# Attention with mirrored score blocks: another order of the key pairs in the middle chunks, later block writes, earlier v loads

## The chip, the cores and the metric

One core of a Trainium2 chip runs the whole program. The metric is the device time of one execution in microseconds; three runs of the kernel before are given, and one profiled execution with its trace. Engines are named as in the profile: PE (matmul), PEld (weight load), DVE (vector), ACT (scalar), POOL and SP (which here issues nearly all DMAs).

## The reference, cut to what matters

```python
# u, v: (8, 2496, 256); z: (8, 2496, 64)
scores = (1.0 / S) * np.matmul(z, z.transpose(0, 2, 1))
attn = np.maximum(scores, 0.0) ** 2
out = np.matmul(attn, v)
x = (u * out).reshape(B * S, D)
# then a mixture of 8 experts over the rows of x: argmax gate, at most 80 rows per expert,
# out[tok] = gate * (relu(x[tok] @ w1[e]) @ w2[e]), the other rows are zero
```

Per batch the matrix of scores is symmetric, since the same z stands on both sides.

## The kernel before

A batch has 2496 rows, padded to 20 tiles of 128 (NT). Queries are taken in 5 chunks of 4 tiles (512 columns, the last 448); keys in 10 pairs of two tiles (NP). A step is one (batch, chunk, pair), 400 in all, and the body of the loop over steps is the program order of PE, ACT, DVE and SP, written out by hand (`manual_schedule`), so each of these engines takes its work in the order in which the loop names it.

For a pair, `scores` (line 301) makes the two operands `ah` and `al` (the squared relu of the scores, rounded, and the rest), two steps ahead of their use (LOOK). There are three kinds of pair in chunk qc:

- *Mirrored*, keys of an earlier chunk j < qc: the block was made transposed when chunk j was the query. ACT casts it from the block `blk` that was read back (line 296), DVE subtracts (line 298, recorded at line 54). PE does nothing.
- *Diagonal*, keys of chunk qc: four score matmuls on PE (lines 312, 313), two relus and a square on ACT (316, 317), cast on DVE (107), subtract on DVE.
- *For later*, keys of a later chunk: the same, with the cast on ACT (line 105; on DVE for the entries of ON_V when b > 0), and `mirror` (line 252): DVE transposes both tiles into `x` (257, pool of NX = 4). After the fourth tile of a block SP writes `x` to DRAM as `y` (261).

The score tiles `s` in PSUM have three banks, two per pair; the operand `a` has two buffers, `ah` and `al` three.

`mirror_back` (265), once per step, reads blocks back with four DMAs each (278) into one of NA = 4 slots, in the order in which they will be used: two steps after their write was issued, at most AHEAD = 12 steps before `scores` uses them, and as soon as a slot is free.

`attend` (330) does a tile's matmuls into the chunk's two accumulators: per half three (343 to 345), for the last tile two (347, 348). A pair is 12 matmuls, the last pair 10.

Beside this each step has extra work at fixed positions r of the chunk: at r = 0 `chunk_x` for the chunk before (DVE, line 362), then ACT's first cast of it (`chunk_hi`, 373); r = 1 the rest on DVE (377) and the transposing store (SP, 412); r = 2 ACT's second cast (381); r = 3 the third part (385); r = 6 the logits (436, 444). The gate of a batch stands in the next batch's chunk 0 at r = 7 (463 to 478) and r = 8 (489 to 504), its counts in chunk 1 at r = 2 and 4 (513, 520). At r = 1 the next batch's z and the next `zd` are loaded (100, 120, 121), at r = 9 `prep_zc` (112). v of the next batch goes through two raw buffers: two loads in chunk 3 at r = 8, casts (146) in chunk 4 at r = 2, 4, 6, 8, 9, each followed by the load of a later group (132). In batch 0 the v groups are loaded and cast in chunk 0. In batch 7 the experts' first weights are loaded and split in chunks 2 to 4 (589, 599, 600).

Of the kernel before, what the change touches and what calls it, by code (L numbers as in the profile page):

```python
# [8 lines left out]
F32 = mybir.dt.float32  # L9
# [16 lines left out]
def attn_moe_kernel(ctx, tc, zT, uT, v, wg, w1, w2, out, seq, cap):  # L26
# [5 lines left out]
    nc = tc.nc  # L32
    V = nc.vector
    B, _, SP = zT.shape
# [3 lines left out]
    NT = SP // P  # L38
# [3 lines left out]
    QT = 4  # L42
    NQ = NT // QT
# [9 lines left out]
    def tt(o, a, b, op):  # L53
        V.tensor_tensor(out=o, in0=a, in1=b, op=op)  # L54
# [9 lines left out]
    dram = ctx.enter_context(tc.tile_pool(name="dram", bufs=1, space=DRAM))  # L64
# [3 lines left out]
    SQ = 32  # L68
# [58 lines left out]
    def load_v(b, g):  # L127
        last = g == NQ - 1
        nf = QT - 1 if last else QT
        raw = zpool.tile([P, QT, D], F32, tag="vraw", name=f"vraw_{b}_{g}")  # L130
        r0 = g * CH
        nc.sync.dma_start(out=raw[:, :nf],
                          in_=v[b, r0:r0 + nf * P, :].rearrange("(t p) d -> p t d", p=P))
        if last:

            r1 = r0 + nf * P
            for h in range(2):
                nc.sync.dma_start(out=raw[h * 64:(h + 1) * 64, nf], in_=v[b, r1:r1 + TAIL, :])
        return raw
# [93 lines left out]
    def zero_out(i, n):  # L233
# [3 lines left out]
                          in_=zero.rearrange("p (o d) -> p o d", o=1).broadcast_to([P, r1 - r0, D]))  # L237


    LOOK, AHEAD = 2, 12  # L240
    a_t = {}

# [1 line left out]

    half_t, y_t, blk, slot_of, free = {}, {}, {}, {}, list(range(NA))
    n32 = P // SQ
    now = [0]

    to_read = [(b, i, j, ((b * NQ + i) * NT + j * QT) // 2 - LOOK)
               for b in range(B) for i in range(NQ) for j in range(i)]  # L250

    def mirror(b, i, j, t, a):

        if t == 0:
            half_t[b, i, j] = sqpool.tile([P, n32, QT, QT, SQ], F32, tag="x", name=f"x_{b}_{i}_{j}")
        x = half_t[b, i, j]
        V.transpose(out=x[:, :, :, t].rearrange("p n k s -> p k n s"), in_=a)  # L257
        if t < QT - 1:
            return
        y = dram.tile([n32, SQ, n32, QT * QT * SQ], F32, tag="y", name=f"y_{b}_{i}_{j}", bufs=12)  # L260
        nc.sync.dma_start(out=y.rearrange("g p h f -> (g p) (h f)"),
                          in_=x.rearrange("p h k t s -> p (h k t s)"))
        y_t[b, i, j] = y, now[0]

    def mirror_back():

# [15 lines left out]
    def pair_tile(tag, b, qc, k, dt=F32R, bufs=3):  # L282
        return ew.tile([P, 2, CH], dt, tag=tag, name=f"{tag}_{b}_{qc}_{k}", bufs=bufs)
# [17 lines left out]
    def scores(b, qc, k):  # L301

        if k // QT < qc:
            return mirrored(b, qc, k)
        nq = min(CH, seq - qc * CH)
        zc, zd = zc_t[b, qc], zd_t[b, qc]
        a = pair_tile("a", b, qc, k, F32, 2)
        ss = []
        for h in range(2):
            zk = zc_t[b, k // QT][:, (k % QT + h) * P:(k % QT + h + 1) * P]  # L310
            s = ps_s.tile([P, CH], F32, tag="s", name=f"s_{b}_{qc}_{k + h}")
            nc.tensor.matmul(s[:, :nq], zk, zc[:, :nq], start=True, stop=False)  # L312
            nc.tensor.matmul(s[:, :nq], zk, zd[:, :nq], start=False, stop=True)  # L313
            ss.append(s)
        for h, s in enumerate(ss):
            nc.scalar.activation(out=a[:, h, :nq], in_=s[:, :nq], func=AF.Relu)  # L316
        nc.scalar.activation(out=a[:, :, :nq], in_=a[:, :, :nq], func=AF.Square)  # L317
        ah = pair_tile("ah", b, qc, k)
        on_v = k // QT == qc or (qc, k) in ON_V and b > 0
        cp(V if on_v else nc.scalar, ah[:, :, :nq], a[:, :, :nq])  # L320
        al = pair_tile("al", b, qc, k)
        tt(al[:, :, :nq], a[:, :, :nq], ah[:, :, :nq], ALU.subtract)
        if k // QT > qc:
            for h in range(2):
                mirror(b, k // QT, qc, k % QT + h, a[:, h])
        a_t[b, qc, k] = (ah, al)
# [2 lines left out]

    def attend(b, qc, k, cols=range(DC)):  # L330
        nq = min(CH, seq - qc * CH)
        if k == 0:
            acc_t[b, qc] = [ps_a.tile([P, CH], F32, tag="acc", name=f"acc_{b}_{qc}_{c}")
                            for c in range(DC)]
        acc = acc_t[b, qc]
        ah, al = (x[:, k % 2, :nq] for x in a_t[b, qc, k - k % 2])
        vt = v_t[b, k // QT]
        t = k % QT
        for c in cols:
            cs = slice(c * P, (c + 1) * P)  # L340
            o = acc[c][:, :nq]
            if k < NT - 1:
                nc.tensor.matmul(o, vt[:, t, 0, cs], ah, start=k == 0, stop=False)  # L343
                nc.tensor.matmul(o, vt[:, t, 1, cs], ah, start=False, stop=False)  # L344
                nc.tensor.matmul(o, vt[:, t, 0, cs], al, start=False, stop=False)  # L345
            else:
                nc.tensor.matmul(o, vt[:, t, 0, cs], ah, start=False, stop=False)
                nc.tensor.matmul(o, vt[:, t, 0, cs], al, start=False, stop=True)


    xt_t, xq_t, lg_t = {}, {}, {}
# [256 lines left out]
        ts(pre["half"], incl[:, :, NBLK - 3], -15.5, ALU.add)  # L608


    NP = NT // 2

    ON_V = {(0, 8), (0, 12), (0, 16)}

    early = [(e, w, part) for e in range(2) for w in (1, 2) for part in range(2)]
    qa, qb, qz = NQ - 3, NQ - 2, NQ - 1
# [4 lines left out]
    WARM = 4, 12  # L621
    steps = [(b, qc, r) for b in range(B) for qc in range(NQ) for r in range(NP)]
    ET = mybir.EngineType
    v_raw, z_raw, w_raw = {}, {}, {}
# [68 lines left out]
    with tc.manual_schedule(engines={ET.PE, ET.Activation, ET.DVE, ET.SP}):  # L693
        prep_zc(0, 0, raw0)
        prep_zd(0, 0, raw0)
        prep_zc(0, 1, raw12[:, 0])
        scores(0, 0, 0)
        prep_v(0, 0, vraw0, nc.scalar, V)
        scores(0, 0, 2)
        v_raw[0, 1] = vraw1  # L700
        z_raw.update({(0, 2): raw12[:, 1], (0, 3): raw34[:, 0], (0, 4): raw34[:, 1]})
        constants()
        prev = None
        for i, (b, qc, r) in enumerate(steps):
            last = b == B - 1 and qc == NQ - 1
            now[0] = i
            if r == 0 and prev:
                chunk_x(*prev)
            if (b, qc) == (0, 0) and r in (0, 2, 4):
                prep_zc(0, r // 2 + 2, z_raw.pop((0, r // 2 + 2)))  # L710
            if i + LOOK < len(steps):
                nb, nqc, nr = steps[i + LOOK]
                scores(nb, nqc, 2 * nr)
            if b == 0 and qc == 0:
                if r % 2 == 0 and r < 8:
                    g = r // 2 + 1
                    prep_v(0, g, v_raw.pop((0, g)), nc.scalar, V)
                    if g + 1 < NQ:
                        v_raw[0, g + 1] = load_v(0, g + 1)
                if r == 8:  # L720
                    constants_v()
            for k in (2 * r, 2 * r + 1):
                if not last or k < NT - 3:
                    attend(b, qc, k)
            if prev:
                finished(*prev, r)

            nb, nqc = (b, qc + 1) if qc + 1 < NQ else (b + 1, 0)
            if r == 2:
                prep_u(b, qc)  # L730
            if b + 1 < B:
                if r == 1:
                    z_raw[b + 1, qc] = load_z(b + 1, qc)
                if r == 9:
                    prep_zc(b + 1, qc, z_raw.pop((b + 1, qc)))
                if qc == NQ - 2 and r == 8:
                    for g in range(2):
                        v_raw[b + 1, g] = load_v(b + 1, g)
                if qc == NQ - 1:
                    g = (r - 1) // 2 if r < 9 else 4  # L740
                    if r in (2, 4, 6, 8, 9):
                        prep_v(b + 1, g, v_raw.pop((b + 1, g)), nc.scalar, V)
                        if g + 2 < NQ:
                            v_raw[b + 1, g + 2] = load_v(b + 1, g + 2)
            if nb < B and r == 1:
                prep_zd(nb, nqc)
            if r == 5:
                zero_out(b * NQ + qc, B * NQ)
            if b == B - 1 and qc >= NQ - 3:
                weights_ahead(qc, r)  # L750
            mirror_back()
            if r == NP - 1:
                prev = b, qc

        chunk_tiles(*prev)
        for kk, c in ((3, 0), (2, 0), (3, 1), (1, 0), (2, 1), (1, 1)):
            attend(*prev, NT - kk, [c])
            if kk == 1:
                chunk_x_last(*prev, c)
        chunk_store(*prev)  # L760
        chunk_logits_last(*prev)
        gate_top(b, NQ - 1, NQ)
        gate(b, NQ - 1, NQ)
        chunk_store2(*prev)
        kb = B * BPB
        count_last(kb - 2, kb)
        blocks(ps_m, "m", gp, oh, kb - 2, kb)
# [546 lines left out]
```

## Time and profile before

| | us |
|---|---|
| three runs, median (lowest to highest) | 1445.17 (1442.82 to 1446.08) |
| the profiled execution's own time | 1441.15 |
| its span on the core | 1439.4 |
| PE busy | 1385.3 (96%) |
| PEld busy | 1135.8 (79%) |
| DVE busy | 1074.9 (75%) |
| ACT busy | 983.1 (68%) |
| mean granted clock of PE | 0.991 |

Attention ends at about 1347 us; the rest is the experts. Busy times are unions of the instructions' recorded spans; ends of matmuls are modelled, so PE can be recorded as busy over short pauses, and pauses are better read from the starts. In the views by stretch, "us" is the length of the stretch, followed by busy time and number of instructions for PE, PEld, DVE, ACT and POOL, the granted clock as a share of full speed, and the busy share and rate of the DMA engines.

### The profile page before, as it was taken

Reading aid. Unit: us, or ns where it says so; the run is one execution under the profiler, and the core shown is the slowest. Engines: PE = TensorE matmul, PEld = TensorE weight load, DVE = VectorE, ACT = ScalarE, POOL = GpSimd, SP = SyncE. Lnnn points to the kernel's source line nnn. Section 1 sums busy time; section 2 is a strip of 40 time slices with the busy share of each in tenths; the row PEclk is TensorE's granted clock in tenths of the full one; section 3 lists DMA queues with packets and bytes.
Section 4 is the critical chain, followed back from the end, with each engine's and each line's share of the span. In section 5 each row is a group of like instructions: output and inputs, shape, how many; then the busy total and the mean of one; then the engine's idle time right before and its main releaser. Section 6 shows DMA issues by size and latency. Waiting matters only on the chain. (4 is left out here: it accounts for less than half of the span.)

```text
span 1439.4 us, 19509 instructions
## 1 busy us (share of the span) xinstructions
PE 1385.3 (96%) x7086; PEld 1135.8 (79%) x7086; DVE 1074.9 (75%) x1530; ACT 983.1 (68%) x1263; POOL 47.5 (3%) x48
## 2 busy tenths in 40 slices
PE   8999999999999999999999999999999999999687
PEld 6788877888788887888788877888878888887466
DVE  7766788667877688677877678767887678766784
ACT  8776677767776587756676577766776667766264
POOL 0000000000000000000000000000000000000075
PEclk9999999999999999999999999999999999999899
DMA  6799978996999959997899959999598979999944
GB/s 203 207 227 223 242 198 209 239 243 157 236 247 222 251 157 216 263 213 210 232 210 237 241 156 235 240 230 259 152 233 237 240 159 238 235 231 253 207 147 134
DMA packets 300103, 311.98 MB, mean 217 GB/s; under 512 B 136184, under 2 KB 228224, under 8 KB 289760
## 3 DMA queue, kind: packets, MB, share of 16 engines
q1 hardware_dynamic: 299040, 309.11, 86.3%
q0 software_dynamic: 960, 1.56, 0.4%
q8 instruction: 57, 0.93, 0.3%
q14 instruction: 46, 0.38, 0.1%
HBM read 153.48 MB, written 126.46 MB: 194 GB/s over the span
## 5 line engine op out<-in xcount | busy, mean ns | idle before, releaser
L345 PE MATMUL acc<-al,vt 128*128 128x512 f32 (+1 forms) x1520 | 587.5, 386 | 7.3 <-DVE al L54 7.1
L343 PE MATMUL acc<-ah,vt 128*128 128x512 f32 (+1 forms) x1520 | 586.9, 386 | 6.3 <-ACT ah L296 4.0
L344 PE MATMUL acc<-ah,vt 128*128 128x512 f32 (+1 forms) x1520 | 586.0, 386 | 1.2 <-DVE vt L146 1.2
L54 DVE TENSOR_TENSOR al<-a,ah 128x1024 fp32r<-128x1024 f32 (+1 forms) x240 | 291.2, 1213 | 143.8 <-ACT ah L105 134.2
L345 PEld LDWEIGHTS acc<-al,vt 128*128 128x128 f32 x1520 | 285.7, 188 | 66.8 <-DVE al L54 14.4
L343 PEld LDWEIGHTS acc<-ah,vt 128*128 128x128 f32 x1520 | 285.8, 188 | 63.5 <-ACT ah L296 7.4
L344 PEld LDWEIGHTS acc<-ah,vt 128*128 128x128 f32 x1520 | 285.9, 188 | 55.1 <-DVE vt L146 2.0
L316 ACT ACTIVATE a<-s 128x512 f32<-128x512 f32 (+1 forms) x480 | 257.6, 588 | 83.1 <-PE s L313 73.4
L296 ACT CAST ah<-blk 128x1024 fp32r<-128x1024 f32 x160 | 166.9, 1048 | 163.0 <-DMA blk<-y 81.7
L54 DVE TENSOR_TENSOR al<-blk,ah 128x1024 fp32r<-128x1024 f32 x160 | 193.0, 1214 | 93.0 <-ACT ah L296 90.5
L317 ACT ACTIVATE a<-a 128x1024 f32<-128x1024 f32 (+1 forms) x240 | 253.0, 1054 | 7.6
L257 DVE STREAM_TRANSPOSE x<-a 128x512 f32<-128x512 f32 x320 | 207.6, 686 | 0.0
L313 PE MATMUL s<-zd,zc 128*128 128x512 f32 (+1 forms) x480 | 186.9, 389 | 0.0
L105 ACT CAST ah<-a 128x1024 fp32r<-128x1024 f32 x139 | 146.0, 1050 | 4.4
L312 PE MATMUL s<-zc,zc 128*128 128x512 f32 x320 | 131.3, 410 | 3.5 <-ACT a L316 3.4
L107 DVE CAST ah<-a 128x1024 fp32r<-128x1024 f32 (+1 forms) x101 | 68.6, 679 | 46.6 <-ACT a L317 46.6
L313 PEld LDWEIGHTS s<-zd,zc 128*128 128x128 f32 x480 | 90.4, 188 | 15.4 <-issue 0.5
L373 ACT CAST xb<-xf 128x1024 bf16<-128x1024 f32 (+1 forms) x39 | 40.1, 1027 | 57.3 <-DVE xf L362 57.2
L312 PEld LDWEIGHTS s<-zc,zc 128*128 128x128 f32 x320 | 60.1, 188 | 21.8 <-ACT a L316 11.8
L312 PE MATMUL s<-zc 128*128 128x512 f32 (+1 forms) x160 | 63.8, 399 | 7.7 <-ACT a L316 7.6
L146 DVE TENSOR_TENSOR vt<-vraw,vt 128x1024 fp32r<-128x1024 f32 (+1 forms) x40 | 46.7, 1167 | 27.8 <-ACT vt L105 27.6
L105 ACT CAST vt<-vraw 128x1024 fp32r<-128x1024 f32 (+3 forms) x56 | 44.9, 828 | 30.9 <-DMA vraw<-v 30.9
(161 smaller groups left out, 843.3 us busy)
## 6 DMA issues: line engine op xcount, KB each, us to landing
y<-x SPq DMA_DIRECT2D x80, 1024.0 KB, 5.4
blk<-y SPq DMA_DIRECT2D x320, 256.0 KB, 8.3
out<-idle SPq DMA_DIRECT2D x40, 512.0 KB, 9.3
vraw<-v SPq DMA_DIRECT2D x32, 512.0 KB, 8.4
ut<-uT SPq DMA_DIRECT2D x32, 512.0 KB, 5.4
xs<-xq SPq DMA_DIRECT2D x32, 512.0 KB, 7.6
wraw<-w SPq DMA_DIRECT2D x28, 512.0 KB, 6.1
zd<-zc SPq DMA_DIRECT2D x78, 128.0 KB, 3.5
```

What stands on the lines that cost most here:

```text
L54: V.tensor_tensor(out=o, in0=a, in1=b, op=op)
L105: eng.copy(out=o, in_=i)
L107: eng.tensor_copy(out=o, in_=i)
L257: V.transpose(out=x[:, :, :, t].rearrange("p n k s -> p k n s"), in_=a)
L296: nc.scalar.copy(out=natural(ah), in_=src)
L312: nc.tensor.matmul(s[:, :nq], zk, zc[:, :nq], start=True, stop=False)
L313: nc.tensor.matmul(s[:, :nq], zk, zd[:, :nq], start=False, stop=True)
L316: nc.scalar.activation(out=a[:, h, :nq], in_=s[:, :nq], func=AF.Relu)
L317: nc.scalar.activation(out=a[:, :, :nq], in_=a[:, :, :nq], func=AF.Square)
L343: nc.tensor.matmul(o, vt[:, t, 0, cs], ah, start=k == 0, stop=False)
L344: nc.tensor.matmul(o, vt[:, t, 1, cs], ah, start=False, stop=False)
L345: nc.tensor.matmul(o, vt[:, t, 0, cs], al, start=False, stop=False)
```

## The change

Chunks 1 to 3 take their pairs in another order: those for later chunks, then the two diagonal ones, then the mirrored ones; chunks 0 and 4 keep theirs. `attend` starts and stops the accumulators at the first and last pair of that order, and `mirror_back`'s due times follow it. The write of a block is named by `mirror_out`, two steps after its last transpose, instead of in `mirror`. The first two v loads of the next batch move from chunk 3's r = 8 to r = 2 and r = 4. ON_V keeps one of three entries, so the casts of pairs 6 and 8 of chunk 0 go from DVE to ACT. Lines that only move are left out.

```diff
+    NP = NT // 2
+    pairs_of = [list(range(NP)) if qc in (0, NQ - 1) else
+                [*range(2 * qc + 2, NP), 2 * qc, 2 * qc + 1, *range(2 * qc)] for qc in range(NQ)]
...
-    now = [0]
-
-    to_read = [(b, i, j, ((b * NQ + i) * NT + j * QT) // 2 - LOOK)
+    now, to_write = [0], []
+
+    to_read = [(b, i, j, (b * NQ + i) * NP + pairs_of[i].index(2 * j) - LOOK)
                for b in range(B) for i in range(NQ) for j in range(i)]
...
-        y = dram.tile([n32, SQ, n32, QT * QT * SQ], F32, tag="y", name=f"y_{b}_{i}_{j}", bufs=12)
-        nc.sync.dma_start(out=y.rearrange("g p h f -> (g p) (h f)"),
-                          in_=x.rearrange("p h k t s -> p (h k t s)"))
-        y_t[b, i, j] = y, now[0]
+        to_write.append((now[0], b, i, j, x))
+
+    def mirror_out():
+
+        while to_write and to_write[0][0] + 2 <= now[0]:
+            _, b, i, j, x = to_write.pop(0)
+            y = dram.tile([n32, SQ, n32, QT * QT * SQ], F32, tag="y", name=f"y_{b}_{i}_{j}", bufs=12)
+            nc.sync.dma_start(out=y.rearrange("g p h f -> (g p) (h f)"),
+                              in_=x.rearrange("p h k t s -> p (h k t s)"))
+            y_t[b, i, j] = y, now[0]
...
-        if k == 0:
+        first, last = 2 * pairs_of[qc][0], 2 * pairs_of[qc][-1] + 1
+        if k == first:
...
-                nc.tensor.matmul(o, vt[:, t, 0, cs], ah, start=k == 0, stop=False)
+                nc.tensor.matmul(o, vt[:, t, 0, cs], ah, start=k == first, stop=False)
                 nc.tensor.matmul(o, vt[:, t, 1, cs], ah, start=False, stop=False)
-                nc.tensor.matmul(o, vt[:, t, 0, cs], al, start=False, stop=False)
+                nc.tensor.matmul(o, vt[:, t, 0, cs], al, start=False, stop=k == last)
...
-    ON_V = {(0, 8), (0, 12), (0, 16)}
+    ON_V = {(0, 8)}
...
-                scores(nb, nqc, 2 * nr)
+                scores(nb, nqc, 2 * pairs_of[nqc][nr])
...
-            for k in (2 * r, 2 * r + 1):
+            p = pairs_of[qc][r]
+            for k in (2 * p, 2 * p + 1):
...
-                if qc == NQ - 2 and r == 8:
-                    for g in range(2):
-                        v_raw[b + 1, g] = load_v(b + 1, g)
+                if qc == NQ - 2 and r in (2, 4):
+                    g = r // 2 - 1
+                    v_raw[b + 1, g] = load_v(b + 1, g)
...
             mirror_back()
+            mirror_out()
```

## Rows read from the trace of the kernel before

**Rows 1.** The page's busy time, share of the span and instructions of each engine.
```profile
PE 1385.3 (96%) x7086; PEld 1135.8 (79%) x7086; DVE 1074.9 (75%) x1530; ACT 983.1 (68%) x1263; POOL 47.5 (3%) x48
```

**Rows 2.** By stretch: chunk 2 of batch 0, chunk 3 of batch 1.
```profile
84.35:117.29 32.94, 32.94 (x168) 27.18 (x166) 23.01 (x29) 23.10 (x29) 0.00 (x0) 1.00 0.86 227
...
283.16:314.29 31.13, 31.13 (x160) 25.68 (x158) 20.45 (x25) 18.59 (x23) 0.00 (x0) 1.00 1.06 221
```

**Rows 3.** By stretch: 36 wide matmuls, then 60 narrow ones.
```profile
616.32:624.48 8.16, 8.16 (x37) 6.76 (x36) 5.83 (x8) 3.03 (x3) 0.00 (x0) 1.00 1.02 222
647.45:659.61 12.16, 12.16 (x62) 11.27 (x60) 10.23 (x12) 7.02 (x7) 0.00 (x0) 1.00 0.98 283
```

**Rows 4.** By stretch: chunk 4, chunks 0 and 1, batch 7's end.
```profile
sum 216.48, PE 207.60 PEld 183.96 DVE 154.94 ACT 141.16 POOL 0.00; mean PE 29.66 PEld 26.28 DVE 22.13 ACT 20.17 POOL 0.00
...
1177.69:1247.35 69.66, 69.64 (x351) 56.52 (x349) 59.53 (x94) 54.34 (x73) 0.00 (x0) 1.00 0.80 200
sum 497.81, PE 491.90 PEld 394.81 DVE 422.89 ACT 379.76 POOL 0.00; mean PE 70.27 PEld 56.40 DVE 60.41 ACT 54.25 POOL 0.00
...
1313.19:1347.00 33.81, 27.74 (x152) 22.66 (x150) 24.97 (x41) 18.30 (x23) 0.00 (x0) 1.00 0.97 238
```

**Rows 5.** Batch 0, order of time (start, us, engine, line); one stretch.
```profile
42.08 0.49 PE L343 MATMUL acc<-ah,vt 128*128 128x512 f32 x1 [2.27 <-ACT vt L105]
...
46.83 0.40 PE L344 MATMUL acc<-ah,vt 128*128 128x512 f32 x1
...
32.59 0.45 SPq L132 DMA_DIRECT2D vraw<-v  x1
...
43.20:46.60 3.40, 3.40 (x9) 2.67 (x10) 1.06 (x2) 3.34 (x4) 0.00 (x0) 0.53 1.09 287
```

**Rows 6.** Who waited for whom, whole span: us in total, times, longest.
```profile
SPq L261 <- DVE x L257: 324.1, 58, 16.4
...
ACT ah L296 <- DMA blk<-y: 81.7, 23, 5.7
```

**Rows 7.** Batch 5, chunk 4, order of time on SP and ACT.
```profile
994.71 0.41 SPq L132 DMA_DIRECT2D vraw<-v  x1
...
1002.14 1.04 ACT L105 CAST vt<-vraw 128x1024 fp32r<-128x1024 f32 x1 [4.98 <-DMA vraw<-v]
```

**Rows 8.** Batch 3, chunks 0 and 1, order of time on ACT.
```profile
544.17 0.34 ACT L467 ACTIVATE ex<-d 128x160 f32<-128x160 f32 x1 [3.07 <-DVE d L54]
...
554.13 1.05 ACT L373 CAST xb<-xf 128x1024 bf16<-128x1024 f32 x1 [3.57 <-DVE xf L362]
555.09 1.08 ACT L316 ACTIVATE a<-s 128x512 f32<-128x512 f32 x2
...
563.76 1.05 ACT L105 CAST ah<-a 128x1024 fp32r<-128x1024 f32 x1
...
566.92 1.05 ACT L105 CAST ah<-a 128x1024 fp32r<-128x1024 f32 x1
```

**Rows 9.** Batch 3, chunks 0 and 1, order of time on DVE.
```profile
541.14 1.23 DVE L54 TENSOR_TENSOR al<-a,ah 128x1024 fp32r<-128x1024 f32 x1 [0.36 <-ACT ah L105]
...
543.50 0.28 DVE L463 TENSOR_REDUCE mx<-lg 128x20 f32<-128x160 f32 x1
...
548.72 0.31 DVE L489 TENSOR_SCALAR_CACHE_REDUCE fw<-d 128x160 f32<-128x160 f32 x1
...
550.56 1.17 DVE L54 TENSOR_TENSOR al<-blk,ah 128x1024 fp32r<-128x1024 f32 x1
...
552.81 1.29 DVE L362 SCALAR_TENSOR_TENSOR xf<-acc,ut 128x512 f32<-128x512 f32 x2
...
570.67 2.02 DVE L54 TENSOR_TENSOR incl<-incl,tot 128x8 f32<-128x8 f32 x10
```

**Rows 10.** Batch 3, chunk 1, order of time on PE.
```profile
547.59 0.50 PE L343 MATMUL acc<-ah,vt 128*128 128x512 f32 x1 [0.69 <-ACT ah L296]
...
555.73 0.50 PE L312 MATMUL s<-zc,zc 128*128 128x512 f32 x1 [0.19 <-ACT a L316]
```

More of the change, by code (lines that the diff above doesn't have):

```diff
@@ L342, in attend @@
             if k < NT - 1:
-                nc.tensor.matmul(o, vt[:, t, 0, cs], ah, start=k == 0, stop=False)
+                nc.tensor.matmul(o, vt[:, t, 0, cs], ah, start=k == first, stop=False)
                 nc.tensor.matmul(o, vt[:, t, 1, cs], ah, start=False, stop=False)
-                nc.tensor.matmul(o, vt[:, t, 0, cs], al, start=False, stop=False)
+                nc.tensor.matmul(o, vt[:, t, 0, cs], al, start=False, stop=k == last)
             else:
                 nc.tensor.matmul(o, vt[:, t, 0, cs], ah, start=False, stop=False)
-                nc.tensor.matmul(o, vt[:, t, 0, cs], al, start=False, stop=True)
+                nc.tensor.matmul(o, vt[:, t, 0, cs], al, start=False, stop=k == last)
     xt_t, xq_t, lg_t = {}, {}, {}
@@ L608, in half @@
         ts(pre["half"], incl[:, :, NBLK - 3], -15.5, ALU.add)
-    NP = NT // 2
-    ON_V = {(0, 8), (0, 12), (0, 16)}
+    ON_V = {(0, 8)}
     early = [(e, w, part) for e in range(2) for w in (1, 2) for part in range(2)]
```

## The prediction

> **What bounds the kernel now.** I read the page's busy times first, then the busy time by stretch, then who waits for whom, then the order of time on each engine around the waits.
>
> PE is busy for 96% of the span [rows 1]. Whether it is the bound in a stage shows in the stretches: chunk 2 takes 32.94 us with 32.94 busy, chunk 3 takes 31.13 with 31.13 busy [rows 2], and so in seven of the eight batches each. There PE issues one matmul after the other, at 0.2267 us for 512 columns (8.16 us by 36) and 0.2027 for 448 (12.16 by 60) [rows 3]. The middle chunks 2 and 3 can therefore give nothing back; a new order there can only add waits. What there is to win lies in four other places:
>
> - Chunk 4 of batches 0 to 6: 216.48 us in all [rows 4]. Unhindered, one would take 126 matmuls of 448 columns (25.54), 12 score matmuls of 512 for the next batch (2.72) and the logits (chunk 3's 31.13 less 134 wide matmuls, 0.75): 29.0. So 13.4 us are waits.
> - Chunks 0 and 1 of batches 1 to 7: 497.81 us; batch 7, which prepares no next batch, takes 69.66 [rows 4]. Seven times that is 487.6, so 10.2 us in batches 1 to 6.
> - Batch 0, where PE waits 2.27 us for the last v tile, and the ten matmul starts from 42.08 to 46.83 take 4.75 us instead of 2.27 [rows 5]. With the wait (2.43 by starts) that is 4.9 us.
> - Chunk 4 of batch 7: 33.81 us with 27.74 busy [rows 4], some 6 us.
>
> Who ends these waits: SP. Its largest wait is for the transposes that a block write needs, 324.1 us in 58 waits, and ACT waits 81.7 us for blocks read back [rows 6]. A block write that waits on SP holds up everything issued behind it. In batch 5 the v load of chunk 4 stands behind a write, the reads that wait for it and the transposes, and is issued only at 994.71; ACT, which takes its instructions in order, stands 4.98 us until 1002.14 for it [rows 7].
>
> **The change, part by part.**
>
> *Block writes two pairs later.* When SP comes to a write, its transposes are done; the 58 waits mostly go. No instruction is added. An x buffer is held two steps longer. It is filled in two steps, then waits two, and there are four buffers, so the next use comes eight steps (29 us) after the first transpose and leaves four steps (14.5 us) for the write to land; I put this at nothing.
>
> *Order of chunks 1 to 3.* The blocks for later chunks are made first, so the last one (4,3) is written in chunk 3's second step and read some seven steps before its use; block (1,0), used first in chunk 1 until now, is used last. The waits for blocks go: the 10.2 us at the start of chunk 1 and part of the 13.4.
>
> *v loads earlier.* Chunk 4's SP queue then holds no block read and two v loads fewer ahead of the third. I take 12.7 of the 13.4 (0.1 left in each batch), and 4.9 in batch 0, where the last v load (32.59 [rows 5]) no longer stands behind a waiting write and four reads. In batch 7 weight loads stand behind the same waits; I take 4 of 6. Bounds for all four places: nothing, if the loads stay late, and 34. I take 31.8, since each wait has a named cause that the change removes.
>
> *What takes the place.* The chunk boundary is now crossed with computed pairs instead of mirrored ones. A mirrored pair costs ACT one cast and DVE one subtract. A pair with transposes costs ACT 3.16 us (cast at 563.76 to cast at 566.92 [rows 8]) and DVE 2.36 (subtract at 541.14 to the next work at 543.50 [rows 9]) against 16 matmuls, 3.63, on PE. ACT has 0.47 us to spare per pair, and the extra work of a boundary has stood beside mirrored pairs so far. Two casts of chunk 0 also go from DVE back to ACT (ON_V); laying them out, the subtract of the pair before the boundary still starts at 541.2, since DVE had been the later one there: nothing.
>
> I lay out the boundary between chunks 0 and 1 in batch 3 by the program order, each instruction at the later of its engine's freedom and its inputs:
>
> 1. ACT's exp of the gate waits 3.07 us for DVE and ends at 544.5 [rows 8]. So far mirrored casts followed. Now pairs 4 and 5 follow: casts done at 547.76 and 550.92.
> 2. DVE: pair 4 from 547.79 (+2.36), the gate (548.72 to 550.56, 1.84), pair 5 (2.36), the next zc (1.17, what 550.56 to 552.81 leaves beside a subtract), then the chunk's x (1.29) [rows 9]: done at 556.84. Before, it was done at 554.1.
> 3. ACT's cast of x (xb) waits for that; already now it waits 3.57 us [rows 8]. It stands between the relus of pairs 6 and 7. With 0.96 for it (554.13 to 555.09) and half of the relus' 1.08, pair 7's first score tile is released at 558.4.
> 4. PE: the row at 547.59 stands 0.86 late (0.69 idle, and by starts 0.17 more) and gets two score groups (1.81) more in front: 548.55. Second tile of pair 5: 0.3 late; subtract of pair 5: 0.4; the second score tile of pair 8 wants the bank of pair 7 at 556.07 and gets it at 558.4: 2.35, and 0.1 to restart. The same wait in the kernel before is the one at 555.73, recorded as 0.19 us idle and 0.46 by starts [rows 10].
> 5. ACT is then late for three pairs: its second cast of x waits for DVE again (0.6 on PE). The diagonal pairs' casts stand on DVE behind the third part of x and the ten sums (2.02 [rows 9]): 1.2 and 0.5.
>
> Sum 5.4 per batch, 32.7 in batches 1 to 6; without the zc work 4.3 in batch 7; without gate and sums 2.0 in batch 0. The same layout gives 1.05 at chunk 2 (both diagonal subtracts behind the x work) in seven batches, 7.4, and about 0.3 at chunk 3, 2.6 with batch 7's weights. Together 49.0. Bounds: below, the boundary costs what the 0.46 us at 555.73 cost so far, about 6 in all; above, each wait of 2.35 also costs clock. I take the laid-out value; it rests on durations of the same instructions one boundary earlier.
>
> **Sum.** 49.0 − 31.8 = +17 us. On the profiled execution, 1441.15, that gives 1458; it lies 4 us under the median of the three runs, 1445.17, and on that the forecast is 1462.
>
> **The clock.** After the wait of 2.27 us in batch 0 the granted clock is 0.53 from 43.20 to 46.60, that is 1.2 GHz in place of 2.4 for nearly all of it [rows 5], and the starts cost 2.48 us more. One case is no pattern, so my sum has no clock cost for the wait of 2.35; it is a rival.
>
> The Trainium skill ("TensorE: Matmul & The Clock Gate", section "HAM oscillation — how this bites in real kernels") says that pauses of PE that recur in a loop put the clock back to half each time. Batch 0's row agrees for one pause; for pauses of this length at each batch no run here shows it.
>
> **Rivals.**
>
> - *Boundaries stay cheap* (ends faster). The place is the cast of x between two relus: if x is done no later than 5.9 us after chunk 1's first attend (556.07 less the 1.55 of step 3, less 548.55), the bank is free in time and nothing is lost. I lay it at 8.3. For it: PE has two pairs of slack, and today a wait of 3.57 us on ACT costs PE only 0.46. Against it: four more transposes stand on DVE in that chain, and ACT starts it 3 us late. Then 31.8 come back and about 6 are paid: 1419.
> - *Half and half.* If the layout is too dark by half (24 instead of 49), 1438; at two thirds (32) no change, 1445.
> - *The clock falls* at six boundaries, at batch 0's price of 2.5, of which later waits absorb some: up to 15 more, 1472.
> - *The loads stay late*: chunk 4 gives only half of its 12.7 and batch 7 nothing, since DMA is busy all through chunk 3 (share 1.06 [rows 2]) and a load issued earlier lands no earlier then. 10 less comes back: 1472. This is also the case in which the change does not do what it says.
>
> **Chances.** Layout holds 0.50; clock 0.10; late loads 0.10; within 0.2% (2.9 us, about what a measurement of this kernel can tell from no change) 0.11; faster, by cheap boundaries or half, 0.19. Slower is then 0.70. The likeliest case alone runs from 1448 (a third off the 49) to 1476 (10 late). The range 1434 to 1476 takes in the half case and leaves out the cheapest boundaries and the darkest sums.
>
> **What would show it.** Right: SP's wait for the transposes falls far under 324 us; ACT's waits for blocks and v tiles nearly vanish; chunk 4 near 29 us; PE waiting on ACT's relu in chunk 1's third step in batches 1 to 7, about 2.4 us in 1 to 6; chunk 2 at about 34 instead of 32.94; chunks 0 and 1 together near 75. Wrong: chunks 0 and 1 at 70 or less, or chunk 2 still at 32.94, would say that the boundary is cheap; chunk 4 still above 30.5 would say that loads and blocks were not late because of SP's queue.

## The result, and the profile after

The changed kernel took 1459.54 us (median of 4 runs, 1456.88 to 1460.11) beside 1444.7 of the kernel before (4 runs, 1442.82 to 1446.08): ratio 1.01, 95% interval 1.0083 to 1.0118. It is slower; the forecast was 1462 in a range of 1434 to 1476. The profiled execution took 1456.88 us at a span of 1455.2; in the kernel before it was 1441.15 at 1439.4.

The page's busy time, which answers to [rows 1]:

```profile
PE 1397.0 (96%) x7085; PEld 1139.2 (78%) x7086; DVE 1066.2 (73%) x1516; ACT 999.6 (69%) x1277; POOL 46.1 (3%) x48
```

PE's share is the same 96% although 16 us were lost: the shares don't show where. The stretches do. First chunk 2 of batch 0 and chunk 3 of batch 1 ([rows 2]); then chunks 0 and 1 of batch 4 and of batch 7, with the sum over batches 1 to 7, and the sum over chunk 4 of batches 0 to 6 ([rows 4]). Columns: from:to, length, then busy time of PE, PEld, DVE, ACT and POOL, granted clock, DMA share, GB/s.

```profile
84.25:118.30 34.05, 33.54 (x167) 27.02 (x166) 22.91 (x28) 22.95 (x29) 0.00 (x0) 1.00 1.00 246
287.25:316.23 28.98, 28.73 (x148) 23.34 (x146) 20.35 (x24) 14.15 (x17) 0.00 (x0) 1.00 1.04 240
...
685.15:761.99 76.84, 74.58 (x363) 59.73 (x361) 59.42 (x94) 60.38 (x81) 0.00 (x0) 0.98 0.78 189
...
1192.89:1268.61 75.72, 73.87 (x363) 58.43 (x361) 58.29 (x92) 60.17 (x81) 0.00 (x0) 1.00 0.80 182
sum 537.35, PE 520.01 PEld 414.09 DVE 414.98 ACT 422.22 POOL 0.00; mean PE 74.29 PEld 59.16 DVE 59.28 ACT 60.32 POOL 0.00
...
sum 205.74, PE 204.48 PEld 184.68 DVE 155.36 ACT 146.69 POOL 0.00; mean PE 29.21 PEld 26.38 DVE 22.19 ACT 20.95 POOL 0.00
```

Chunk 4 got shorter, from 216.48 to 205.74 us in seven batches. Chunk 2 went from 32.94 to 34.05, and chunks 0 and 1 from 497.81 to 537.35 in seven batches. Of these 39.5 us, 19.0 are no loss: the new order moves 12 score matmuls per batch from chunk 3 (28.98 us now, 31.13 before) to chunks 0 and 1, 2.72 us at the pitch of [rows 3].

Who waited for whom (us in total, times, longest): SP's wait for the gate, the rows that answer to [rows 6], and the wait for v tiles:

```profile
SPq L513 <- DVE gall L511: 107.0, 8, 14.4
...
SPq L272 <- DVE x L262: 47.7, 16, 7.2
...
ACT ah L307 <- DMA blk<-y: 26.6, 14, 4.8
...
ACT vt L105 <- DMA vraw<-v: 11.2, 7, 3.1
```

SP waits 47.7 us for transposes in place of 324.1, ACT 26.6 us for blocks in place of 81.7 and 11.2 us for v tiles in place of 30.9. A part of SP's waiting only moved: in front of the gate's two writes it now waits 107.0 us for DVE (37.5 before). What came instead stands around the boundary from chunk 0 to 1. In batch 3, the order of time on ACT ([rows 8]), then on DVE ([rows 9]), then on PE ([rows 10]):

```profile
546.70 0.34 ACT L479 ACTIVATE ex<-d 128x160 f32<-128x160 f32 x1 [3.06 <-DVE d L54]
...
555.45 1.05 ACT L105 CAST ah<-a 128x1024 fp32r<-128x1024 f32 x1
559.15 1.04 ACT L385 CAST xb<-xf 128x1024 bf16<-128x1024 f32 x1 [2.65 <-DVE xf L374]
560.11 1.08 ACT L327 ACTIVATE a<-s 128x512 f32<-128x512 f32 x2
```

```profile
552.58 0.28 DVE L501 TENSOR_SCALAR_CACHE_REDUCE fw<-d 128x160 f32<-128x160 f32 x1
...
554.39 1.16 DVE L54 TENSOR_TENSOR al<-a,ah 128x1024 fp32r<-128x1024 f32 x1
555.47 1.29 DVE L262 STREAM_TRANSPOSE x<-a 128x512 f32<-128x512 f32 x2
556.69 0.39 DVE L112 CAST zc<-zraw 128x512 fp32r<-128x512 f32 x1
557.11 0.69 DVE L54 TENSOR_TENSOR zc<-zraw,zc 64x512 fp32r<-64x512 f32 x1
557.83 1.29 DVE L374 SCALAR_TENSOR_TENSOR xf<-acc,ut 128x512 f32<-128x512 f32 x2
```

```profile
560.75 0.50 PE L323 MATMUL s<-zc,zc 128*128 128x512 f32 x1 [2.12 <-ACT a L327]
...
562.81 0.63 PE L357 MATMUL acc<-al,vt 128*128 128x512 f32 x1
563.24 0.63 PE L355 MATMUL acc<-ah,vt 128*128 128x512 f32 x1
```

The chain is the one laid out. DVE still has the gate, a subtract, two transposes and the next zc ahead of x, which is ready at 559.1. ACT, with nothing to do from 556.5, waits for it with its cast (xb), and the relus that would free PE's score bank stand behind that cast. PE waits 2.12 us. Behind the wait, matmuls start 0.43 us apart in this batch.

### The profile page after: what moved, and what is told of

Its sections match the earlier page's. It is cut to its first block, busy times and chain, and to the rows that moved or that the text cites. A ratio compares the mean times of both kernels' runs of the same rounds, so it can differ in the third digit from the quotient of the medians.

```text
span 1455.2 us, 19460 instructions
## 1 busy us (share of the span) xinstructions
PE 1397.0 (96%) x7085; PEld 1139.2 (78%) x7086; DVE 1066.2 (73%) x1516; ACT 999.6 (69%) x1277; POOL 46.1 (3%) x48
## 5 line engine op out<-in xcount | busy, mean ns | idle before, releaser
L357 PEld LDWEIGHTS acc<-al,vt 128*128 128x128 f32 x1520 | 287.2, 189 | 82.8 <-DVE al L54 30.4
L105 ACT CAST ah<-a 128x1024 fp32r<-128x1024 f32 x153 | 160.7, 1050 | 4.8
L323 PE MATMUL s<-zc,zc 128*128 128x512 f32 x320 | 128.1, 400 | 15.4 <-ACT a L327 15.3
L107 DVE CAST ah<-a 128x1024 fp32r<-128x1024 f32 (+1 forms) x87 | 58.9, 676 | 45.4 <-ACT a L328 45.4
L323 PEld LDWEIGHTS s<-zc,zc 128*128 128x128 f32 x320 | 60.2, 188 | 34.2 <-ACT a L327 22.5
L393 ACT CAST xb<-xr 128x1024 bf16<-128x1024 f32 (+1 forms) x39 | 40.1, 1027 | 47.4 <-DVE xr L54 47.4
```

What stands on the lines that cost most here:

```text
L105: eng.copy(out=o, in_=i)
L107: eng.tensor_copy(out=o, in_=i)
L357: nc.tensor.matmul(o, vt[:, t, 0, cs], al, start=False, stop=k == last)
```

## The experiments

Runs on one chip shared their runs of the kernel before, whose median was 1434 to 1445 us from chip to chip, so kernels are compared by their ratio to it. The first four expectations (order_back, onv_three, xcast_later, gate_late) are in us on the scale of the result above, where the kernel before took 1444.7; beside those four runs it took 1434.1, so some 10 us have to be taken off them. In the chunks, "step 3" is the one with r = 3.

### Which part of the change loses

**order_back**: the changed kernel with natural order.

```
-    pairs_of = [list(range(NP)) if qc in (0, NQ - 1) else
+    pairs_of = [list(range(NP)) if True else
```

> The changed kernel with every chunk in natural order; block writes two steps later, v loads earlier and ON_V with one entry stay. Theory (the boundary waits come from the order alone, the waits of chunk 4 and batch 0 were made by the queue): chunks 0 to 3 as in the kernel before or better, batch 0's 4.9 us back; but block (4,3) is written two steps later than before and read later still, so chunk 4 waits for it: 3 to 5 us in each batch on top of nothing else, 1440 to 1460 in all, with chunks 2 and 3 back at 32.94 and 31.13 and chunk 1 under 36. Rival (the later writes or the v loads slow the kernel, not the order): chunk 1 and 2 stay long, 1458 or more.

Measured: ratio 1.0001 (0.9978 to 1.0024). The loss is the order's. But the change's other parts bring nothing on balance either: chunks 0 and 1 are down to 485.27 us in batches 1 to 7 (497.81 before), while chunk 4 rose to 230.28 (216.48). In the natural order the last block, (4,3), is made at the end of chunk 3 and read in chunk 4, and the write two pairs later makes it come later still. Its waits, from the view of who waited for whom:

```profile
ACT ah L307 <- DMA blk<-y: 39.4, 7, 7.8
...
PE acc L355 <- ACT ah L307: 13.5, 8, 3.2
```

**onv_three**: the changed kernel with the two casts of chunk 0 on DVE, as before.

```
-    ON_V = {(0, 8)}
+    ON_V = {(0, 8), (0, 12), (0, 16)}
```

> The changed kernel with ON_V as before (casts of pairs 4, 6 and 8 of chunk 0 on DVE). Theory: DVE then starts the boundary later by about the two casts' 1.6 us less what ACT gains, so equal to slightly slower, 1458 to 1466. Rival 1 (the two casts moved back to ACT make the changed kernel slow): 1445 to 1450.

Measured: ratio 1.0133 (1.0107 to 1.016), chunk 1 at 40.0 us as in the changed kernel. The casts are not the cause; "nothing" was the right price.

### Which wait it is

**xcast_later**: x is cast one step later; ACT then has the relus of another pair to do before it needs x.

```
-        if r == 0:
+        if r == (0 if at_end else 1):
             chunk_hi(b, qc)
-        elif r == 1:
+        if r == 1:
             chunk_rest(b, qc)
```

> The changed kernel with one edit: ACT's first cast of a finished chunk (chunk_hi) is named one step later, behind the relus, square and cast of the next pair. Theory (the cast waits for DVE's x and holds back the relus whose score banks PE needs): PE's wait of 2.1 us idle at chunk 1's third score group and the half-speed matmuls behind it go, 6 times about 2.5 + 1.4 and once 1.3; some comes back at the diagonal pairs: 1438 to 1446 where the changed kernel takes 1459.5. Rival 1 (ACT has too much to do in chunks 0 and 1 because of the casts moved back to it): ACT's work is the same, so 1457 to 1461. Rival 2 (DVE is the bound there, whatever ACT's order): the wait moves to PE's wait for DVE's subtract, 1453 to 1460.

Measured: ratio 0.9954 (0.9939 to 0.9968), on the same chip 26 us under onv_three (1427.48 and 1453.46), more than the 14 to 22 of the theory. It is faster than both kernels. The same place in batch 3, on ACT:

```profile
545.46 1.05 ACT L105 CAST ah<-a 128x1024 fp32r<-128x1024 f32 x1
546.86 1.09 ACT L327 ACTIVATE a<-s 128x512 f32<-128x512 f32 x2 [0.35 <-DVE x L262]
...
550.03 1.04 ACT L385 CAST xb<-xf 128x1024 bf16<-128x1024 f32 x1
```

The relus no longer stand behind the cast, and the cast no longer waits. Step 1 of chunk 1 falls from 6.3 to 3.9 us, and chunk 2 to 32.94, chunk 3 to 28.4: their costs, too, were the cast of x in front of the relus, and this is what the theory had left out.

**gate_late**: the other end of the chain. The gate of a batch moves from the end of chunk 0 to chunk 2, where DVE has more room.

```
-            if r == 7:
-                gate_top(b, 0, NQ)
-            elif r == 8:
-                gate(b, 0, NQ)
...
+        if qc == 1 and b > 0:
+            if r == 4:
+                gate_top(b - 1, 0, NQ)
+            elif r == 5:
+                gate(b - 1, 0, NQ)
+            elif r == 6:
                 count(*part)
```

> The changed kernel with the gate of the batch before and its counts and sums moved from chunk 0 (steps 7, 8) and chunk 1 (steps 2, 4) to chunk 2 (steps 4 to 7, beside mirrored pairs); the logits tile gets a second buffer. Theory (extra work stands beside computed pairs at the boundary): without ACT's hold of 3.1 us at the exp and DVE's 1.84 and 2.05, chunks 0 and 1 take in every batch what they take in batch 0 (73.9) or a little less, in place of 76.9: 3 us in each of 7 batches, 1435 to 1442. Rival 1 (ACT's casts): 1455 to 1460. Rival 2 (the order itself costs, with or without the gate): less than 8 us back, 1452 to 1458.

Measured: ratio 1.0157 (1.0131 to 1.0184); the expected gain is missing. Yet the theory of the boundary held: without the gate in the chain, chunk 1 takes 36.3 us though the cast is early. The time went to chunk 2, which takes 37.3 to 39.95 us in batches 1 to 7 (34.04 to 34.09 in the changed kernel, 32.98 in batch 7). In batch 4, where it is longest, by stretch (chunks 1 and 2), then on PE and on DVE:

```profile
722.31:758.60 36.29, 35.50 (x176) 28.45 (x174) 25.67 (x32) 27.16 (x35) 0.00 (x0) 1.00 0.89 235
758.60:798.55 39.95, 36.65 (x173) 29.23 (x172) 27.82 (x52) 23.59 (x32) 0.00 (x0) 0.91 0.96 195
```

```profile
784.56 0.29 PE L523 MATMUL tp<-oh,ones_b 128*128 128x80 bf16 x2 [2.77 <-DVE lg L456]
```

```profile
782.84 0.28 DVE L511 RECIPROCAL gall<-s 128x20 f32<-128x20 f32 x1
783.11 1.23 DVE L54 TENSOR_TENSOR al<-blk,ah 128x1024 fp32r<-128x1024 f32 x1
784.26 0.25 DVE L456 TENSOR_REDUCE lg<-pl 128x32 f32<-128x96 f32 x1
```

I had put the counting matmul into the step of the chunk's own logits. It needs the PSUM space that DVE frees when it sums them, and this sum now stands behind the gate and two subtracts (in the kernel before, the gate came two steps after the logits' step and the count four steps after the gate). PE stood 2.77 us with its attends queued behind. I had moved a wait, not removed it.

### Which part gains

**v_back** and **writes_now**: xcast_later with one part of the change undone each.

```
-                if qc == NQ - 2 and r in (2, 4):
-                    g = r // 2 - 1
-                    v_raw[b + 1, g] = load_v(b + 1, g)
+                if qc == NQ - 2 and r == 8:
+                    for g in range(2):
+                        v_raw[b + 1, g] = load_v(b + 1, g)
```

> The changed kernel with the cast of x a step later, and the first two v loads of a batch issued in chunk 3's step 8 again, as in the kernel before. Theory: it was the order that freed chunk 4 (the last block is written early in chunk 3, so SP's queue is empty when the loads come to it), and the place of the v loads is worth little: chunk 4 stays at 29.1 to 29.5 us, and the ratio is 0.995 to 0.998. Rival, the prediction's own step: the loads were late because of their place; then chunk 4 rises by 2 us or more in batches 0 to 6 and the ratio is 1.004 or more.

```
-        to_write.append((now[0], b, i, j, x))
+        to_write.append((now[0] - 2, b, i, j, x))
+        mirror_out()
```

> The changed kernel with the cast of x a step later, and each block written as soon as its transposes are named, as in the kernel before. Theory: SP waits for transposes again (250 us or more over the span in place of some 48), but with the new order nothing urgent stands behind these waits, so that chunk 4 stays at 29.1 to 29.8 us and the ratio is 0.995 to 0.999. Rival, the prediction's step: SP's wait is what made the loads late; then v tiles and blocks come late in chunk 4 again, it takes more than 30.5 us, and the ratio is 1.003 or more.

Measured: v_back 0.9985 (0.997 to 1.0), writes_now 0.9958 (0.9944 to 0.9972), against 0.9954. The early v loads are worth some 0.3%: without them ACT waits 37.0 us for v tiles instead of 8.6, and chunk 4 takes 214.03 us in seven batches instead of 204.57. That lies between my theory and its rival. The later writes are worth nothing that can be measured: SP waits 199.1 us for transposes again, and chunk 4 is at 206.73. With the new order nothing urgent stands behind those waits.

**nat_late**: order_back with xcast_later's edit.

> The changed kernel with every chunk in its natural order again and the cast of x a step later; with three earlier runs it fills a square of order and cast. Theory: the late cast has a worth only where the new order has put computed pairs on the chunk boundary; among mirrored pairs the cast of x had slack. Then the ratio to the kernel before is 0.997 to 1.000 (natural order with the early cast gave 1.0001), chunk 1 gains at most 0.5 us per batch (from 34.59 to 34.1), and chunk 4 stays at 31 to 36 us. Rival: a late cast is good under any order; then the ratio is about 0.986, as the late cast was worth 1.45% under the new order.

Measured: ratio 1.0094 (1.0077 to 1.0111). Chunk 1 gained 0.3 us, as expected, and chunk 4 stayed between 30.4 and 36.5. So the late cast brings a gain only under the new order. Why the ratio is above order_back's is open: the profiled run, at 1442.74 us, was the fastest of five with a median of 1453.2, and what its trace has more than order_back's is above all chunk 4, where ACT waits for blocks (235.49 us in seven batches, 230.28 there), and whose length varies by 5 to 6 us between the batches of either kernel.

### What the slow matmuls cost

**keep_warm**: the changed kernel with nine matmuls on zeros in the wait of step 1.

```
                 nb, nqc, nr = steps[i + LOOK]
+                if b > 0 and (qc, r) == (1, 1):
+                    warm(9, ps_m, "m")
```

> The changed kernel with nine added matmuls of 512 columns on zeros, whose result nobody reads, in front of the score matmul that waits 2.12 us in chunk 1's step 1 of batches 1 to 7; they fill the wait. Theory: the granted clock no longer falls behind the wait, the seven to nine starts at 0.43 us come at 0.23, and that is time won, 1.0 to 1.5 us in four to six batches: ratio to the kernel before 1.004 to 1.007, where the changed kernel has 1.010. Rival: what the slow matmuls cost, the later waits of chunk 1 for DVE's subtracts would have taken anyway: the clock stays up, chunk 1 stays within 0.4 us of 40.03, and the ratio is 1.009 to 1.011.

Measured: ratio 1.014 (1.0118 to 1.0162). By stretch, first the changed kernel, chunk 1 of batch 3 and the slow matmuls in it:

```profile
551.36:591.32 39.96, 37.66 (x180) 29.62 (x179) 30.06 (x53) 29.84 (x39) 0.00 (x0) 0.96 0.95 191
...
562.38:565.79 3.41, 3.41 (x12) 2.45 (x10) 2.40 (x4) 3.35 (x5) 0.00 (x0) 0.55 0.97 240
```

then chunk 1 of batch 1 of the same execution and the wait on PE in it:

```profile
213.18:253.16 39.98, 36.94 (x180) 28.34 (x179) 30.06 (x53) 29.63 (x39) 0.00 (x0) 1.00 0.96 196
```

```profile
222.57 0.50 PE L323 MATMUL s<-zc,zc 128*128 128x512 f32 x1 [2.08 <-ACT a L327]
```

and the kernel with the wait filled, batch 3:

```profile
551.61:591.56 39.95, 38.60 (x190) 29.23 (x189) 30.05 (x53) 29.60 (x39) 0.00 (x0) 1.00 0.92 205
```

The clock stays at 1.00, and chunk 1 takes 39.95 us instead of 39.96. So the rival holds for the chunk's length; the ratio itself lies a little above its 1.009 to 1.011. PE gets to the next relu and the next subtract earlier and waits there (0.19 us idle in step 3 and 0.59 in step 6, which batch 3 of the changed kernel did not have). The changed kernel shows the same without any added matmul: in batches 1 and 5 the clock stayed at 1.00 behind a wait of 2.08 us, in batches 2, 3, 4 and 6 it fell, and chunk 1 takes 39.98 and 40.31 us in the former, 39.93 to 39.98 in the latter. The length of this chunk is set by the chain over ACT and DVE, whatever PE's clock does.

**after_again**: the changed kernel once more, on the chip that ran nat_gate below.

> The changed kernel, unaltered, beside the kernel before on the chip of this call. The kernel before took 1434 to 1445 us from call to call, the kernels with the changed order and the early cast 1453 to 1459.5. Theory: the changed kernel waits for its own engines and hardly varies from chip to chip, while the kernel before waits for transfers and does; then this run takes 1452 to 1460 us whatever the kernel before takes, and the ratio moves with the latter, 1.010 to 1.015. Rival: the ratio is a property of the two kernels: 1.008 to 1.012 on this chip too.

Measured: 1451.25 us, ratio 1.0115 (1.0083 to 1.0147). The interval holds both answers, so this decides nothing between them. Beside it, keep_warm's 1454.92 us (ratio 1.014, on another chip, the kernel before at 1434.08 and 1433.77) shows no gain from keeping the clock up.

### A version that beats both

**gate_mid**: xcast_later with the gate in chunk 3 and three steps before its matmul.

```
+        if qc == 2 and b > 0:
+            if r == 4:
+                gate_top(b - 1, 0, NQ)
+            elif r == 5:
+                gate(b - 1, 0, NQ)
+            elif r == 8:
+                count(*part)
+            elif r == 9:
+                up_to(*part)
```

> The changed kernel with the cast of x a step later and the gate of a batch moved from the end of chunk 0 and chunk 1 into chunk 3 (gate at steps 4 and 5, sums and counts only at steps 8 and 9). Theory: what is left of the loss at the boundary (chunk 1 at 37.99 us with the late cast alone, 36.31 with the gate in chunk 2) is DVE's gate work standing ahead of the subtracts; in chunk 3 DVE is busy 20.3 of 28.4 us, and with three steps between the gate and the matmul that needs it PE no longer waits (2.77 us idle where only one step lay between). Chunks 0 and 1 then take 73 us together in place of 74.8, chunk 3 stays under 29, and the ratio is 0.987 to 0.991. Rival: the gate costs the same wherever it is put, since each subtract behind it is late by its length: chunk 3 rises to about 30 and the ratio stays within 0.993 to 0.997.

Measured: ratio 1.0077 (1.006 to 1.0094). Neither theory: chunks 0 to 3 ran as hoped (36.57, 34.75, 32.94, 28.78 in batch 4), and chunk 4 took it all back (34.2 to 37.5 us in batches 1 to 6). Stretch of chunk 4 in batch 4, then SP and ACT in order of time:

```profile
811.54:849.08 37.54, 32.31 (x166) 28.41 (x164) 23.89 (x33) 21.41 (x28) 0.00 (x0) 0.91 0.93 182
```

```profile
802.52 8.17 SPq L513 DMA_DIRECT2D xs<-gall  x2
810.73 1.23 SPq L236 DMA_DIRECT2D out<-idle  x1
812.06 7.96 SPq L289 DMA_DIRECT2D blk<-y  x8
```

```profile
825.49 1.04 ACT L307 CAST ah<-blk 128x1024 fp32r<-128x1024 f32 x1 [8.87 <-DMA blk<-y]
```

The gate's two small writes occupy SP for 8.17 us, and the reads of the last two blocks stand behind them.

**gate_mid_sp**: the same, with those writes issued in chunk 4.

```
+        if qc == 3 and b > 0 and r == 7:
+            gate_store(b - 1, 0, NQ)
```

> The kernel with the gate in chunk 3, with one thing changed: the two writes of the gate's weights are issued in chunk 4's step 7 instead of right behind the gate. Theory: with the gate in chunk 3, chunks 0 to 3 ran without waits (36.57, 34.76, 32.94, 28.76 us), and chunk 4 gave it back because these two writes stood on SP for 8.17 us, waiting for DVE, with the last two block reads behind them (issued at 812.06, in the kernel with only the late cast at 798.09 of a batch that began some 8 us earlier). With the writes out of the way chunk 4 falls from 35.7 to 29.0 to 29.8 us, six batches gain 5 to 6.5 us each, and the ratio to the kernel before is 0.978 to 0.986. Rival: the blocks are late because the DMA engines are full from chunk 1 on (share 0.88 to 0.99), so that whatever PE gains earlier it waits for in chunk 4: chunk 4 stays over 33 us and the ratio is 1.002 to 1.009.

Measured: 1411.26 us beside 1434.08, ratio 0.984 (0.9815 to 0.9866): faster than both kernels. SP in batch 4, then the stretches of chunks 0 to 4 there:

```profile
784.12 9.41 SPq L289 DMA_DIRECT2D blk<-y  x8
```

```profile
660.55:697.11 36.56, 36.56 (x183) 30.18 (x182) 29.09 (x39) 32.69 (x44) 0.00 (x0) 1.00 0.69 212
697.11:731.87 34.76, 34.76 (x176) 28.67 (x175) 25.66 (x32) 27.19 (x35) 0.00 (x0) 1.00 0.88 235
731.87:764.81 32.94, 32.94 (x168) 27.17 (x167) 22.92 (x28) 22.98 (x29) 0.00 (x0) 1.00 0.99 251
764.81:793.56 28.75, 28.75 (x153) 23.46 (x151) 23.27 (x39) 14.58 (x18) 0.00 (x0) 1.00 0.94 234
793.56:822.63 29.07, 29.07 (x166) 26.50 (x164) 23.81 (x33) 21.37 (x28) 0.00 (x0) 1.00 1.06 200
```

The reads are out before chunk 4 begins, and in each chunk PE is busy for the whole stretch: 162.1 us per batch, 166.6 in batches 2 to 6 of the kernel before. The DMA share of 1.06 in chunk 4 didn't hinder, so the rival falls.

**nat_gate**: gate_mid_sp in the natural order with prompt writes (the edits of order_back and writes_now together).

> The fastest kernel so far (late cast, gate in chunk 3, its writes in chunk 4) with two parts of the change undone: every chunk in its natural order, and each block written as soon as its transposes are named. It asks what the new order itself is worth once the boundary is clear. Theory: it is worth what chunks 1 and 4 wait for blocks in the natural order: block (4,3) is written at the end of chunk 3 and read in chunk 4, so chunk 4 takes 31 us or more in place of 29.1, and chunks 0 and 1 wait for block (1,0); 2 to 5 us per batch, ratio to the kernel before 0.990 to 1.000 against 0.984. Rival: the late cast, the moved gate and the early v loads do it alone, and the order is worth nothing: chunk 4 at 29.1 to 29.6 and the ratio within 0.982 to 0.987.

Measured: ratio 1.0019 (1.0004 to 1.0033) against 0.984, a little beyond the theory's 1.000. Chunks 0 and 1 run clear in batches 1 to 7, but batch 0's chunk 0 takes 39.95 us (36.83 there), chunk 4 takes 31.7 us on average in batches 2 to 6 instead of 29.1, and SP waits 308.2 us for transposes. Chunk 4 is the largest part of the difference: 221.22 us in seven batches, 204.01 in gate_mid_sp. Two parts are undone here at once, so the difference belongs to the order and the later writes together; that it is the order's rests on writes_now, where the later writes alone measured nothing. The order was a good idea; what it was paid with could be avoided.

## Why the prediction was right

Net change by place, in us over the batches named, with the 12 moved score matmuls (2.72 us per batch) counted in chunk 3:

```
place                           predicted            measured
chunks 0, 1, batches 1 to 6     32.7 - 10.2 = 22.5   17.2
chunks 0, 1, batch 7            4.3                  3.3
chunks 0, 1, batch 0            2.0 - 4.9 = -2.9     -2.7
chunk 2                         7.4                  7.7
chunk 3                         2.6                  3.9
chunk 4, batches 0 to 6         -12.7                -10.7
chunk 4 of batch 7 and the end  -4                   -2.7
sum                             17                   16
```

The measured column is the stretch of after less that of before; the first line is 461.63 - 428.15 - 6 x 2.72. That the sum comes out within a microsecond or so is partly luck: chunks 0 and 1 of batches 1 to 7 cost 6.3 us less than laid out, and the other lines together 5.1 us more.

- **The boundary.** The order of events was right: x was laid out for 556.84; the batch now runs 2.5 us later (the gate's exp starts at 546.70, not 544.17), which makes 559.4, and x came at 559.1. PE's wait, laid out at 2.35 us, was 2.12 idle. It stands in chunk 1's second step; the prediction said the third. If the 10.2 came back in full, the 5.4 per batch was 0.9 too much, and it is the later terms (0.6, 1.2 and 0.5) that were mis-sized: in their place batch 3 has seven starts at 0.43 instead of 0.23 us, 1.4 in all, and one wait of 0.17 us for a subtract; batch 1, without slow starts, has waits of 0.19, 0.60 and 0.17. That the chain is what decides is shown from both ends: chunk 1 of batch 4 takes 39.95 us in the changed kernel, 37.93 with the late cast, 36.29 with the moved gate and 34.75 with both.
- **The 10.2 us.** The prediction gave them to the new order. order_back, in the natural order, has them back as well: chunks 0 and 1 of batches 1 to 6 take 416.16 us there, 12.0 less than in the kernel before. So the later writes, the early v loads or the casts moved to ACT are enough for it; which of them, no run separates.
- **Chunk 2.** 1.05 per batch laid out, 1.1 measured. The cause was named wrongly in part: both diagonal subtracts do stand behind the x work, but xcast_later shows that a later cast alone clears them.
- **Chunk 4.** 10.7 of 12.7 came back. Five of seven batches reach 29.05; batches 3 and 5 still waited for a block (4.83 us on ACT in batch 3). v_back shows that the v loads' place had a part; under the new order SP's waits have hardly one, as writes_now shows. The step "the 58 waits mostly go" was right for the waits named, while SP's wait at the gate's writes grew by 69.5 us; under the new order it was worth nothing by itself. ACT's waits for blocks and v tiles fell to about a third (81.7 to 26.6 and 30.9 to 11.2 us), they did not "nearly vanish".
- **Batch 7's chunk 4.** 2.7 of 4: ACT there waits 1.82 us for a weight tile in front of the relus, a load the change does not move.
- **Boundaries that stay cheap, half the cost, late loads**: none happened. Chunks 0 and 1 at 76.9 us (the prediction's "near 75" had forgotten the moved score matmuls) exclude the first.
- **The clock.** Half of this rival happened. The starts at 0.43 us with a low granted clock (0.55 in batch 3) came back in batches 2, 3, 4 and 6, as the row of batch 0 had it once; in batches 1 and 5 the clock stayed up behind the same wait. The Trainium skill ("TensorE: Matmul & The Clock Gate", section "HAM oscillation — how this bites in real kernels") says that recurring pauses put the clock back each time; these rows agree in four of the six batches. But the price of 2.5 us per boundary was wrong: keep_warm shows nothing lost. Leaving the clock out of the sum was right, for a reason the prediction didn't have.
- **Side sums.** Two figures beside the forecast are off: 15 us on 1462 make 1477, not 1472, and with a third off the 49 the kernel would take 1446, not 1448. The forecast and its range do not rest on them.

## What to carry to other kernels

When work is reordered so that a boundary is crossed with dearer items, lay out the in-order queues around it instruction by instruction: here that gave a net loss of 17 us where 16 were measured, and it names the instruction to move, here a cast that waited in front of work that was ready. Ask of every moved step what stands behind it on each queue, small DMA issues included: gate_late and gate_mid both cleared the boundary and gave the time back elsewhere. A change that measures slower can still be the better base, once the one wait it creates is moved.

## What the runs showed of the hardware

- How long a DMA issue holds SP differs by several times for the same transfer. The second of the gate's two writes (10 KB each, in packets under 512 bytes) occupied SP for 1.19 to 1.54 us in all seven batches of the changed kernel, where the DMA engines had been idle, and for 7.64 to 8.51 us in all seven of gate_mid, where they were full. By stretch just before such a pair of writes, first in the changed kernel (written at 725), then in gate_mid (at 802.5), then in gate_mid_sp (at 815.6); the DMA share is the last column but one:

```profile
720.00:725.00 5.00, 5.00 (x23) 4.10 (x22) 3.91 (x11) 4.93 (x7) 0.00 (x0) 1.00 0.00 0
```

```profile
795.00:802.50 7.50, 7.50 (x42) 6.04 (x41) 6.94 (x19) 2.67 (x5) 0.00 (x0) 1.00 1.04 268
```

```profile
810.58:815.58 5.00, 5.00 (x47) 4.50 (x46) 3.78 (x6) 3.20 (x5) 0.00 (x0) 1.00 1.10 302
```

  Full DMA engines alone are not the cause: in gate_mid_sp the pair held SP for only 2.26 us behind the third row, and for 2.06 to 3.05 in batches 1 to 6, with shares of 0.90 to 1.13 in the five us before. In the kernel before it was 5.68 to 6.49 us, at shares of 1.03 to 1.05. What the issue waits for stays open. My expectation for gate_mid_sp put the 8.17 us down to a wait for DVE. The reciprocal that the writes need ended at 802.49 and the first was issued at 802.52, so SP was held by the issue itself.
- A pause of 2.1 us on PE can be enough for the granted clock to fall behind it (in batch 3 to 0.55 over 3.4 us, that is 1.2 GHz for nearly all of them): it fell in four batches of the changed kernel (2.08 to 2.12 us idle) and did not in two (2.08). The loss was hidden whole by another chain.
